# One of two small additions between two segments goes from VectorE to GpSimd, in a kernel whose order of work is written out by hand

## The chip, the cores and the metric

The kernel runs on one core of a Trainium2 chip. The metric is device time in microseconds (us) of one execution. Before the change three runs took 830.95, 831.56 and 833.34 us; the median is 831.56. One further execution was profiled: it took 830.06 us, and its span from the first to the last instruction is 828.3 us.

## The reference

Two attentions over the same 2048 rows of 512 values are mixed by a gate for each row. Part A is recurrent: the rows are cut into 64 segments of 32, and in front of each stand 8 memory rows, which are the first 8 output rows of the segment before it. Nothing of a segment that uses its memory rows can start before the segment before it has been projected out.

```python
mem = mem0                                     # (1, 8, 512)
for s in range(n_seg):                         # 64 segments of 32 rows
    h = jnp.concatenate([mem, x[:, 32*s:32*(s+1), :]], axis=1)
    q, k, v = (jnp.einsum('btd,dhe->bhte', h, W) for W in (Wq, Wk, Wv))   # 32 heads of 128
    scores = jnp.einsum('bhqe,bhke->bhqk', q, k) * scale
    p = softmax(jnp.where(mask, scores, -1e9))
    o = jnp.einsum('bhte,hed->btd', jnp.einsum('bhqk,bhke->bhqe', p, v), Wo)
    mem = o[:, :8, :]
    outs.append(o[:, 8:, :])
```

Part B is an attention over four blocks of 512 rows with 32 heads of 16, causal within a block, with a linear memory over the blocks before. The output is `g * a + (1 - g) * b`.

## The kernel before

**Start.** The first 60 us load the inputs, project part B for three of its four blocks, transpose x and store parts in DRAM. What follows, some 750 us, is the recurrence of part A with part B and the remaining work laid into its gaps.

**Order.** `A_ORDER` (L1069) is a text of 4589 units in the order in which they are recorded. Every unit is a small function that appends instructions to the queues of the engines; each engine then runs its own queue in that order, and semaphores hold it until its inputs are there. So the text sets the order on every engine at once. A `~` behind a unit that evacuates PSUM sends it to ScalarE instead of VectorE, or the other way (`evac`, L380 to L385).

**A segment.** In `segment(s)` the units are:
- `K0x` to `V1y`: the projections, by weight (K, Q, V), half of the heads (0, 1) and half of the contraction (x, y). Eight matmuls of 512 columns each (L1292); for Q1, sixteen of 256 (L1514). `k0`, `q0`, `v0` evacuate them and `TK0`, `TQ0` transpose (L1304).
- `Z`, `S`, `X`, `Y`, `M`, `L`, `N`, `n`: bias of the mask (L1560), scores (L1574), exponential (L1588), mask, sums (L1607), reciprocal (L1614, L1617), normalisation on VectorE (L1621) and of the memory rows on GpSimd (L1626).
- `PV`: probabilities times values (L1638, L1649). `E0` to `E3` evacuate it. `W0` to `W3` multiply by the output weights (L1375), sixteen matmuls each.
- `hm`: the memory rows for the next segment (`w_mem`, L1673). W leaves even and odd contributions in PSUM, in two halves of the partitions. A transpose (L1675) brings them into `tt`, a copy (L1676) brings partitions 64 to 127 of it to 0 to 63 in `tu`, and two additions (L1680, `hma` and `hmb`) of 64 partitions by 32 values write their sums into `xTp`: one for partitions 0 to 63, one for 64 to 127. All four are on VectorE. The first projection of the next segment waits for both additions.
- `H`, `ws`: the 32 output rows, evacuated and sent to DRAM.

**Work beside it.** `L` units are the projections of the memory rows' queries of four segments at a time, `O` their output parts, `T` the mix and the output of 128 rows (`T.b` is its matmul, L1455; `T.a` its sum on GpSimd, L1442). `pj` and `pp` project part B's fourth block. `bS` is two steps of part B's scores on TensorE (L932), `bE` an exponential on ScalarE (L953) followed by a causal select on GpSimd (L959), `bP` a step of its values (L985), `bT` the steps behind them (L1056 among them, on GpSimd). `oL` and `qt` are copies on GpSimd (L1704, L1727), `xl` too (L1317).

**GpSimd's queue.** `P.op` makes each GpSimd operation wait for the one before it (L116, L117). It runs strictly one after another in the recorded order.

A wait is recorded for the last writer of each tile that is read (`_mk_deps`); the two halves of a segment's memory rows are two names, `xu` and `xt`, and a projection reads both:

```python
rx = x_res(v, s // 16) + [Rs("xt%d" % s), Rs("xu%d" % s)]
```

Of the kernel before, what the change touches and what calls it, by code (L numbers as in the profile page):

```python
# [867 lines left out]
class BAttn:  # L868
# [210 lines left out]
    pj 2.E2~ pj pp pp 2.W0 2.W1 2.W2 2.W3 2.hm bP bS bP pj 3.qt pj 3.Q0x 3.Q0y bE bE 3.q0 bE 3.K0x~ 3.K0y 3.TQ0 3.K1x 3.K1y~ bE 3.Q1y 3.k0~ 3.TK0 3.Q1x
    3.S0 3.V0x 3.q1y~ 3.k1 3.TK1 1.ws 3.q1x 3.TQ1y 3.Z1 3.X0 2.H 3.TQ1x 3.V1x 3.Y0 3.S1~ bP 3.X1 3.M0 pp~ 3.V0y~ 3.L0 3.n0 3.M1 bP 2.oL bS 3.v0 3.L1 3.n1  # L1080
    3.V1y~ bE 3.N0 2.ws 3.N1 3.v1 pj bE pj 3.PV bT bE 3.E1~ L1.VL1x 3.E0~ L1.VL1y bE 3.W0 pp 3.E3 3.W1 3.E2~ 3.W2 L1.VL1e~ 3.W3 bS 4.qt 3.hm pj pj L1.VLt
    3.H bP pp bT bT bP bE bE 4.Q0x~ bE 4.Q0y~ 4.K0x~ 4.K0y~ bE 4.Q1y 4.q0~ 4.K1x 4.K1y 4.Q1x 4.k0~ bP 4.TK0 3.ws bP 4.TQ0 4.q1y~ 4.S0~ bS 4.k1 4.q1x~
    4.TK1 4.TQ1x 4.X0 L2.xl 4.V1x~ 4.TQ1y bE 4.Y0 4.Z1 bE 4.V1y~ 4.S1~ 4.M0 bE 4.X1 4.V0x~ 4.v1 4.V0y~ 4.M1 pj 4.L0 4.v0 pj 4.L1 pj 3.oL 4.n0 4.n1 4.N0
    4.N1 4.PV~ pj bE 5.Z1 4.E0 pp 5.qt 4.E1 bP 4.W0 pp~ 4.E2 4.W1 4.W2 4.E3~ 4.W3 bS~ bP O0.0 4.oL O0.1 4.hm bE 5.K0x~ 5.K0y~ bE bT 5.Q0x~ bE bE 5.k0
    5.Q0y~ 4.H 5.K1x~ 5.K1y 5.TK0 5.Q1y 5.q0~ 5.k1 bT 5.TQ0 5.TK1 5.Q1x 5.S0 5.V0x~ 5.q1y 5.q1x 5.TQ1y 5.TQ1x 5.X0 5.V0y 5.S1 5.X1 5.Y0 5.V1x~ 5.M0 5.V1y~
    5.L0 5.n0 5.M1 5.v0 O0.2 5.L1 5.v1 L2.KL1x 5.n1 5.N0 5.N1 O0.3 5.PV bP 5.E2~ 4.ws L2.KL1y~ O0.e bP 5.E0 6.qt bS~ 5.E1~ 5.W0 5.E3 L2.KL1e~ 5.W1 5.W2
    O0.s bE 5.W3 L2.KL0x 5.hm L2.KL0y~ bE bE bE bS~ bP 5.H bP 6.K0x~ 6.Q0x L2.KL0e bE bE bT bE 6.Q1y~ 6.K0y bE 6.k0~ 6.Q0y~ 6.Q1x~ 6.q1y~ 6.q1x~ 6.TQ1y
    6.TK0 bS~ bP 6.q0~ bP 6.K1x bE bE 6.TQ1x 6.TQ0 6.K1y 6.k1~ 6.TK1 6.V0x~ 6.S0~ 6.V1x~ bE 6.X0 6.Z1 6.Y0 bT 6.V0y~ bE 6.v0 6.S1 6.X1 6.M0 6.V1y~ 6.M1
    6.L0 6.n0 6.L1 bP 6.v1 bP bS~ 6.n1 5.oL 6.N0 6.N1 bE 6.PV~ bE 7.qt L2.QL1x bE bT 6.E0~ L2.QL1y 6.E1~ 6.E3 5.ws 6.E2 6.W0 L2.QL1e bE 6.W1 6.W2 6.W3 bP
    bP bS~ bE 6.hm L2.QL0x bE L2.QL0y 7.Q1x~ 7.K0x L2.QL0e 7.K0y~ 6.H bT 7.q1x~ bE 7.Q0x 7.k0 7.TK0 7.Q0y 7.K1x~ 7.K1y~ bE 7.q0~ 7.k1 7.TQ0 7.Q1y bP bP  # L1090
    7.q1y 7.S0 bS~ 7.TQ1x 7.TK1 7.X0 7.Z1 7.V1x 6.oL 6.ws 7.TQ1y bE bE bT 7.S1~ 7.V1y~ 7.X1 7.V0x bE 7.Y0 7.M0 7.V0y~ bT 7.M1 7.v1 7.L0 7.v0 7.N0 7.n0
    L2.VL0x 7.L1 L2.VL1x L2.VL0y 7.n1 7.N1 7.PV 7.E2~ L2.VL1y bE L2.VL0e~ 7.E1~ 7.E0 bP L2.VL1e 8.qt bP bS 7.W0 bE 7.E3 7.W1 7.W2 bE bE 7.W3 bE 8.Z1
    L2.VLt bS~ 7.hm 7.H bP bP bE bT bT bE 8.Q0x bE 8.Q0y 8.q0 8.K0x 8.K0y 8.K1x bE 8.k0 8.K1y 8.k1 8.TQ0 8.Q1y 8.TK0 8.Q1x 8.S0~ 8.V0x~ 8.V0y~ 8.q1y 8.TK1
    8.TQ1y 8.q1x 8.X0 8.TQ1x 8.S1 8.Y0 9.Z1 L3.xl 7.oL 8.X1 8.M0 8.v0 8.V1x 8.M1 8.V1y 8.L0 8.L1 8.N0 8.N1 L3.KL1x 7.ws 8.v1~ 8.n0 8.n1 O1.0 8.PV~ 8.E0
    8.E1~ 8.E3 bP L3.KL1y~ L3.KL1e 8.W0 9.qt 8.W1 8.E2 8.W2 8.W3 bP bS 8.hm 8.oL O1.1 O1.2 8.H bE 9.Q1x 9.K0x~ 9.K0y bE bE 9.Q0x~ 9.Q0y~ 8.ws 9.K1x~ bE
    9.k0~ 9.q1x 9.K1y~ bP 9.TQ1x 9.q0~ 9.Q1y 9.TK0 9.k1 9.TQ0 9.q1y 9.S0 9.TK1 9.TQ1y 9.V1x 9.V1y 9.X0 9.Y0 9.v1 9.S1~ 9.X1 bP 9.M0 9.L0 9.V0x~ 9.N0 9.M1
    9.L1 10.qt 9.n0 9.V0y~ O1.3 9.v0~ 9.N1 9.n1 O1.e~ L3.KL0x 9.PV bT 9.E0 9.E1~ 9.E3 bT L3.KL0y 9.W0 9.E2 9.W1 O1.s 9.W2 9.W3 11.Z1 bT bS~ 9.hm L3.QL0x
    L3.KL0e~ bE 10.Z1 L3.QL0y~ bE 10.K0x 10.Q0x~ bE 10.K0y~ 9.H 10.Q0y 10.K1x~ L3.QL0e 10.q0~ 10.k0~ 10.TQ0 10.K1y~ 10.Q1x~ 10.k1 10.Q1y 10.TK0 10.q1x
    9.oL 10.S0~ 10.V0x 10.TK1 10.q1y 10.TQ1x 10.V0y 10.X0 bE 10.TQ1y 10.S1 10.V1x 10.Y0 10.M0 9.ws 10.V1y~ 10.X1 10.L0 10.M1 10.L1 10.v0 T0.l 10.v1 10.N0
    L3.QL1x 10.n0 10.n1 10.N1 L3.VL0x L3.VL0y 10.PV bP 10.E0 L3.VL0e L3.QL1y 10.W0 10.E1 10.W1 10.E2 L3.QL1e~ 10.W2 10.E3~ 10.W3 10.hm bT bP bS T0.b bE  # L1100
    11.K0x~ bE 11.K0y~ 11.qt 11.Q0x~ 10.H 11.k0~ bE 11.Q0y~ bE 11.K1x~ 11.K1y 10.oL 11.Q1x~ T0.a 11.TK0 11.q0 11.TQ0 11.k1 11.TK1 11.q1x 11.Q1y~ 10.ws
    11.S0~ 11.q1y 11.TQ1x 11.V1x~ 11.X0 11.V0x 11.TQ1y 11.S1 T0.t 11.Y0 11.M0 bP 11.V0y~ 11.X1 11.L0 11.M1 bS 11.v0 11.L1 11.n1 11.N0 bP 11.N1 11.n0
    11.V1y bE L3.VL1x bE 11.v1 11.PV~ bE 11.E0 11.E1 11.E2~ 11.E3~ L3.VL1y 11.W0 L3.VL1e~ 11.W1 11.W2 11.W3 bE 11.hm 11.H L3.VLt bS 12.qt bP 11.ws bT bP
    bE bT bT bE 12.Q1x 12.K0x 12.K0y bE 12.Q1y bT 12.Q0x~ 12.q1x 12.Q0y 12.TQ1x bE bT 12.K1x~ 12.K1y~ 12.k0 bP bP bS~ 12.q1y L4.xl 12.q0~ 12.TK0 12.k1
    12.TQ0 bE 12.Z1 12.S0 12.X0 12.TQ1y bE 12.TK1 12.Y0 12.V0x~ 12.S1~ 12.V1x 12.M0 11.oL 12.V1y 12.X1 12.M1 12.V0y L4.KL1x 12.L0 12.L1 12.n0 12.v1 12.N0
    L4.KL1y 12.N1 T0.f 12.n1 12.v0~ 12.PV bE 12.E0 12.E3 L4.QL1x 12.E1~ 12.W0 12.W1 12.E2~ 12.W2 12.W3 L4.KL1e~ L4.KL0x 13.qt L4.KL0y 14.Z1 13.Z1 12.hm
    L4.KL0e~ L4.QL1y~ L4.QL1e~ 13.Q0x 13.Q0y~ 13.q0~ 13.K0x 12.H 13.K0y~ 13.TQ0 13.k0 bE 13.K1x 13.Q1x~ 13.q1x 13.TK0 13.K1y~ 13.S0~ 13.Q1y~ 13.TQ1x
    13.V1x~ 13.k1 13.TK1 13.q1y bP 13.V1y 13.TQ1y 13.S1~ 13.X0 bP 13.Y0 12.ws 13.M0 12.oL 13.V0x~ 13.X1 13.L0 13.M1 13.v1 13.n0 13.V0y O2.0 13.L1 13.N0
    13.n1 13.N1 O2.1 13.v0~ 13.PV L4.QL0x 13.E3~ 13.E1~ L4.QL0y 13.E0~ 13.W0 13.W1 13.E2~ L4.QL0e~ 13.W2 13.W3 bS 13.hm bE O2.2 bE bT bT 14.qt O2.3 14.K0x
    bE O2.e T1.l 14.Q0x 14.K0y~ 13.oL 14.Q0y bE 14.K1x 14.K1y~ 14.Q1x 14.k0~ 14.TK0 14.q0~ 14.TQ0 14.Q1y 14.S0 15.Z1 14.V1x 14.k1 14.q1x~ 14.TK1 14.V1y  # L1110
    14.TQ1x 14.q1y 14.TQ1y 14.S1 14.X0 T1.a 14.Y0 14.V0x 14.X1 14.M0 O2.s 14.V0y~ 14.M1 14.v1 13.H~ 14.L0 14.v0 L4.VL0x 14.N0 L4.VL0y 14.n0 14.L1 14.N1
    L4.VL1x 14.n1 14.PV~ L4.VL0e~ 14.E0 L4.VL1y 14.E1~ 14.E3 14.E2~ 13.ws L4.VL1e~ bT bT bT 14.W0 15.qt 14.W1 14.W2 14.W3 bP T1.b bP bS~ 14.hm 14.H bE bE
    15.Q0x 15.Q0y~ 15.q0 15.K0x~ T1.t bE 15.K0y~ 15.K1x 15.K1y~ 15.Q1y 15.TQ0 bE 15.k0~ 15.Q1x 15.k1 15.q1y 15.TK0 15.q1x 15.TK1 15.S0~ 15.V0x~ 15.X0
    15.TQ1y 15.TQ1x 14.oL 15.V0y 15.Y0 15.S1~ bP 15.M0 15.v0 15.V1x~ 15.X1 bP 15.M1 15.L0 15.L1 15.V1y 14.ws L5.xl 15.N0 15.v1 15.N1 15.n0 15.n1 bS bT bE
# [675 lines left out]
```

## Time and profile before

| | |
|---|---|
| median of three runs | 831.56 us (830.95 to 833.34) |
| profiled execution, its span | 830.06 us, 828.3 us |
| busy: TensorE, weight loads | 786.0 us, 486.1 us |
| busy: VectorE, ScalarE, GpSimd | 583.2, 562.7, 290.0 us |
| granted TensorE clock | 0.999 |
| the transpose in `hm` (L1675), 63 times | 450 ns each |
| the copy in `hm` (L1676), 63 times | 217 ns each |
| the two additions (L1680), 126 times | 207 ns each |

A busy time is the union of an engine's instructions. TensorE has two rows in the profile: PE, the matmuls, and PEld, the loading of the stationary operand, which runs ahead of the matmuls. In a group of instructions the columns are the busy time, the mean duration of one in ns, and the idle time of the engine just before them with what ended it. In a timeline the columns are the start and the duration in us.

### The profile page before, as it was taken

To read this page: it belongs to the slowest core of one execution; us is meant where nothing else is said; L and a number is where in the kernel's file an instruction comes from. 1 tells how busy PE (TensorE), PEld (TensorE's weight loads), DVE (VectorE), ACT (ScalarE), POOL (GpSimd) and SP (SyncE) were. 2 spreads that over 40 slices of the span, in tenths; PEclk is the share of its full clock that TensorE was granted. 3 is DMA by queue.
4 is the path that set the end of the run, shared out by engine and by line. 5 is a ranking of instruction groups with operands and counts; after the bars stand their busy time and mean duration, and the time that the engine had idled before them with its cause. 6 is when DMAs were issued, how large, how long until landed. Compare 5 with 4: busy or idle time off the path is not lost.

```text
span 828.3 us, 50504 instructions
## 1 busy us (share of the span) xinstructions
PE 786.0 (95%) x22701; PEld 486.1 (59%) x22707; DVE 583.2 (70%) x1486; ACT 562.7 (68%) x1353; POOL 290.0 (35%) x727
## 2 busy tenths in 40 slices
PE   9988999999999989999999999999999999999996
PEld 4644566656565656555556656556655656556565
DVE  4547676777677767787757677878667777787654
ACT  5544776867757677775767767776586685787543
POOL 4602442432435233242332434334133332454211
PEclk9999999999999999999999999999999999999999
DMA  8996332122213122112113122121312112120321
GB/s 330 417 377 193 97 94 70 53 50 69 65 59 82 30 63 61 48 34 79 51 49 91 32 60 70 25 62 41 88 57 62 54 59 65 33 72 17 87 87 59
DMA packets 100596, 72.28 MB, mean 87 GB/s; under 512 B 58036, under 2 KB 94492, under 8 KB 98844
## 3 DMA queue, kind: packets, MB, share of 16 engines
q1 hardware_dynamic: 99676, 68.24, 26.9%
q8 instruction: 178, 2.92, 1.5%
q10 hardware_dynamic: 704, 0.80, 0.3%
q14 instruction: 38, 0.31, 0.1%
HBM read 43.43 MB, written 25.58 MB: 83 GB/s over the span
## 4 chain that ended last, share of the span: by engine, by line
PE 77%; ACT 7%; DVE 6%; POOL 3%; DMA 3%; issue 3%; SPq 0%; DVEq 0%; POOLq 0%; ACTq 0%
PE ps L1292 38%; PE ps L1375 15%; PE ps L1514 6%; PE ps L1638 3%; PE ps L932 2%; PE ps L985 2%; ACT PTT L953 2%; POOL PTT L959 2%; DMA scr_kqd<-stgk 2%; PE ps L698 1%; PE ps L1574 1%; PE ps L1455 1%; DMA Wv_sb<-in_A_Wv_dram 1%; PE ps L1607 1%; ACT R_sb L1617 1%
## 5 line engine op out<-in xcount | busy, mean ns | idle before, releaser
L953 ACT ACTIVATE PTT<-ps 128x512 bf16<-128x512 f32 x320 | 172.2, 602 | 51.9 <-PE ps L932 37.6
L959 POOL TENSOR_SCALAR_AFFINE_SELECT PTT<-PTT 128x128 bf16<-128x128 bf16 (+2 forms) x320 | 121.2, 379 | 242.2 <-ACT PTT L953 223.5
L1292 PE MATMUL ps<-Wv_sb,xTp 128*32 128x512 bf16 x2048 | 145.4, 382 | 0.4 <-issue 0.4
L1292 PE MATMUL ps<-Wk_sb,xTp 128*32 128x512 bf16 x2048 | 133.3, 379 | 1.3 <-DVE xTp L1680 0.9
L1375 PE MATMUL ps<-Wo_sb,OT_sb 128*32 128x256 bf16 x4096 | 125.6, 273 | 9.4 <-ACT OT_sb L383 4.6
L1375 PEld LDWEIGHTS ps<-Wo_sb,OT_sb 128*32 128x32 bf16 x4096 | 104.3, 97 | 32.7 <-ACT OT_sb L383 23.0
L1626 POOL TENSOR_TENSOR P_sb<-P_sb,R_sb 128x64 bf16<-128x64 bf16 x128 | 50.3, 393 | 170.5 <-ACT R_sb L1617 165.4
L1292 PEld LDWEIGHTS ps<-Wk_sb,xTp 128*32 128x32 bf16 x2048 | 57.0, 97 | 51.1 <-DVE xTp L1680 5.8
L383 ACT ACTIVATE QN_sb<-ps 128x256 bf16<-128x256 f32 (+1 forms) x152 | 67.3, 445 | 28.1 <-PE ps L1292 23.2
L383 ACT ACTIVATE OT_sb<-ps 128x320 bf16<-128x320 f32 x157 | 59.0, 438 | 30.6 <-PE ps L1649 29.2
L383 ACT ACTIVATE KN_sb<-ps 128x512 bf16<-128x512 f32 x88 | 52.8, 600 | 31.1 <-PE ps L1292 30.4
L385 DVE CAST V_sb<-ps 128x512 bf16<-128x512 f32 x82 | 56.0, 685 | 24.3 <-PE ps L1292 22.7
L1514 PE MATMUL ps<-Wq_sb,xTp 128*32 128x256 bf16 x2048 | 72.1, 273 | 0.7 <-DVE xTp L1680 0.5
L1304 DVE STREAM_TRANSPOSE KT_sb<-KN_sb 128x256 f32<-128x256 f32 x128 | 55.9, 437 | 21.6 <-ACT KN_sb L383 17.6
L1292 PE MATMUL ps<-Wq_sb,xTp 128*32 128x512 bf16 x1024 | 70.6, 379 | 0.4 <-DVE xTp L1680 0.3
L1304 DVE STREAM_TRANSPOSE QT_sb<-QN_sb 128x128 f32<-128x128 f32 (+1 forms) x192 | 63.1, 335 | 8.2 <-ACT QN_sb L383 6.4
L1588 ACT ACTIVATE P_sb<-ps 128x224 bf16<-128x224 f32 x128 | 45.7, 357 | 32.3 <-PE ps L1579 30.9
L1675 DVE STREAM_TRANSPOSE tt<-ps 128x256 f32<-128x256 f32 x63 | 28.4, 450 | 53.6 <-PE ps L1375 52.8
L1514 PEld LDWEIGHTS ps<-Wq_sb,xTp 128*32 128x32 bf16 x2048 | 55.4, 97 | 17.4 <-DVE xTp L1680 3.9
L385 DVE CAST OT_sb<-ps 128x320 bf16<-128x320 f32 x99 | 44.6, 485 | 24.8 <-PE ps L1649 23.6
L1292 PEld LDWEIGHTS ps<-Wv_sb,xTp 128*32 128x32 bf16 x2048 | 44.7, 100 | 14.3 <-issue 1.6
L1621 DVE TENSOR_TENSOR P_sb<-P_sb,R_sb 128x160 bf16<-128x160 bf16 x128 | 40.2, 330 | 12.1 <-ACT R_sb L1617 11.5
(146 smaller groups left out, 1409.9 us busy)
## 6 DMA issues: line engine op xcount, KB each, us to landing
scr_aTd<-WN SPq DMA_DIRECT2D x63, 128.0 KB, 2.4
AR<-scr_aTd SPq DMA_DIRECT2D x60, 96.0 KB
Wk_sb<-in_A_Wk_dram SPq DMA_DIRECT2D x4, 1024.0 KB, 10.4
Wq_sb<-in_A_Wq_dram SPq DMA_DIRECT2D x4, 1024.0 KB, 13.9
Wv_sb<-in_A_Wv_dram SPq DMA_DIRECT2D x4, 1024.0 KB, 13.5
Wo_sb<-in_A_Wo_dram SPq DMA_DIRECT2D x8, 512.0 KB, 6.2
scr_vld<-VNL SPq DMA_DIRECT2D x16, 256.0 KB, 2.3
VL<-scr_vld SPq DMA_DIRECT2D x64, 64.0 KB
```

The costliest lines, as they stand in the source:

```text
L383: P.op("act", lambda a: a.activation(dst, src, ACT.Copy), reads=[v.rbank[k] for k in bks], writes=dres, name=name)
L385: P.op("dve", lambda d: d.tensor_copy(dst, src), reads=[v.rbank[k] for k in bks], writes=dres, name=name)
L953: P.op("act", lambda a: a.activation(pt, v.pb[bk], ACT.Exp, scale=v.SCALE_B), reads=[v.rbank[bk]], writes=[rp], name="be%d_%d" % (n, t))
L959: P.op("gp", lambda g: g.affine_select(mv, mv, [[0, len(cut)], [1, 128]], ALU.is_ge, 0.0, base=0, channel_multiplier=-1), reads=[rp], writ ...
L1292: ins = pe.matmul(pb[bk][SEG * j:SEG * (j + 1), :], lhs(c), cols(w, j) if split else w[:, 512 * j:512 * (j + 1)], start=(c == 0), stop=(c ...
L1304: P.op("dve", lambda d: d.transpose(to, src), reads=reads, writes=writes, name=name)
L1375: ins = pe.matmul(pb[bk][SEG * j:SEG * (j + 1), 0:256], lhs(h), Wo_sb[:, h, :].rearrange("p (k q c) -> p q k c", q=2, c=64)[:, j % 2], sta ...
L1514: ins = pe.matmul(pb[bk][SEG * j:SEG * (j + 1), 0:256], lhs(c), cols(w_sb[:, c, 2048 * b + 1024 * half:2048 * b + 1024 * (half + 1)], j), ...
L1588: P.op("act", lambda a: a.activation(P_sb[:, b, :], pb[bk][:, 0:So], ACT.Exp, scale=SCALE), reads=[rbank[bk]], writes=[Rs("Pm%d" % b), Rs( ...
L1621: P.op("dve", lambda d: d.tensor_tensor(wide[b][:, :, 0:L], wide[b][:, :, 0:L], R_sb[:, b, :].rearrange("p (i q) -> p i q", q=L), ALU.mult ...
L1626: P.op(ENG["n"], lambda d: d.tensor_tensor(left, left, grp04(R_sb[:, b, :]), ALU.mult), reads=[Rs("R0_%d" % b)], writes=[Rs("PL%d" % b)], ...
L1675: P.op("dve", lambda d: d.transpose(v.tt[:, :, :].rearrange("p (k n) t -> p k n t", n=2), src), reads=[rbank[wb["bk"]]], writes=[Rs("tt")] ...
```

## The change

In `w_mem` the second of the two additions is recorded for GpSimd instead of VectorE. Its operands are the same. The transpose, the copy and the first addition stay on VectorE.

```diff
             for b in range(2):
                 dst = xTp[64 * b:64 * b + 64, :, SEG * (s + 1):SEG * (s + 1) + M].rearrange("p (a n) t -> p a n t", n=2)
                 one, two = (t[0:64, :, 0:M].rearrange("p (a b n) t -> p b a n t", a=2, b=2)[:, b] for t in (v.tt, v.tu))
-                P.op("dve", lambda d, dst=dst, one=one, two=two: d.tensor_tensor(dst, one, two, ALU.add), reads=[Rs("tt"), Rs("tu")], writes=[Rs("x%s%d" % ("ut"[b], s + 1))], name="hm%s%d" % ("ab"[b], s))
+                P.op(("dve", "gp")[b], lambda d, dst=dst, one=one, two=two: d.tensor_tensor(dst, one, two, ALU.add), reads=[Rs("tt"), Rs("tu")], writes=[Rs("x%s%d" % ("ut"[b], s + 1))], name="hm%s%d" % ("ab"[b], s))
```

`A_ORDER` is a new text. It has the same 4589 units, apart from the `~` marks (902 before, 886 after), in another order from its fourth line on. As an example, this is what stands between `W3` and the first projection of the next segment at three of the 63 boundaries:

```diff
-28.W3 L8.KL1y~ bS 28.hm bP O6.0 28.H bE L8.KL1e bE bE bT 29.Q1y~
+28.W3 28.hm L8.KL0e~ L8.KL1e~ bS~ bT 29.Z1 bP O6.0 28.H bE bE 29.Q1y~
-46.W3 bS 47.Z1 L12.QL1x L12.QL1y~ bE 46.hm 47.K0x
+46.W3 47.qt bT bS~ 47.Z1 46.hm L12.QL1y~ bE L13.xl 47.K0x~
-56.W3 L15.KL1x 56.hm bT bT L15.KL1y~ L15.KL0e~ bP bP bS 56.H L15.KL1e~ 57.Q0x~
+56.W3 bT bP L15.KL1y 56.hm bS L15.KL0e~ 56.H L15.KL1e~ bT bP 57.K0x
```

Counted over all 63 boundaries, the units between `W3` and the first projection are, before and after: half projections of `L` 58 and 54, `O` 35 and 34, `pj` 7 and 6, `T.b` 9 and 9, `bS` 50 and 50, `bP` 58 and 47, `Z` 28 and 23. Between `W3` and `hm` alone, `bE` stands 28 times before and 20 times after. Between the last of `V0y` and `V1y` and `PV`, half projections of `L` are 74 before and 80 after.

More of the change, by code (lines that the diff above doesn't have):

```diff
@@ L1079 @@
[L1079 to L1114, printed above, removed]
@@ L1256 @@
+    63.K0y 63.Q0y 63.Q1y 62.ws 63.k0~ 63.K1x O15.s 63.K1y 63.q0~ 63.TK0 T15.l 63.q1y 63.V0x~ 63.TQ1x 63.TQ0 63.k1~ 63.S0~ 63.TK1 63.V1x~ 63.V0y~ 63.X0
+    63.Y0 63.M0 63.TQ1y 63.S1~ T14.t 63.L0 63.V1y 63.v0 63.X1 63.v1~ 63.n0 63.M1 63.L1 T14.f 63.N0 63.n1 T15.b 63.N1 63.PV~ 63.E0 63.E1 63.E3 63.E2 T15.a
+    63.W0 63.W1 63.W2 63.W3 T15.t 63.H T15.f
 """
```

325 lines of the change are left out of this document (179 added, 146 removed).

## The prediction

> **What bounds the kernel now.** I read the page's busy table first, then the chain that ended last, then the groups by line, and then one segment boundary in the timeline.
>
> ```profile
> span 828.3 us, 50504 instructions
> PE 786.0 (95%) x22701; PEld 486.1 (59%) x22707; DVE 583.2 (70%) x1486; ACT 562.7 (68%) x1353; POOL 290.0 (35%) x727
> PE 77%; ACT 7%; DVE 6%; POOL 3%; DMA 3%; issue 3%; SPq 0%; DVEq 0%; POOLq 0%; ACTq 0%
> L1680 DVE TENSOR_TENSOR xTp<-tt,tu 64x32 bf16<-64x32 f32 x126 | 26.0, 207 | 3.0
> ```
>
> TensorE is busy for 786.0 of 828.3 us, so all its idle time is 42.3 us, and no cheaper vector operation can win more than that. The two additions together cost VectorE 26.0 us, but VectorE holds only 6% of the chain that ended last. What counts is when they end, because the first projection of the next segment waits for them. The view of one line shows who waited:
>
> ```profile
> L1680 DVE TENSOR_TENSOR xTp<-tt,tu x126: 182/184/1260, 76.0 to 812.4; 64x32 bf16<-64x32 f32 x126
>   PEld ps L1292: 9.8, 29
>   PEld ps L1514: 3.9, 10
> ```
>
> Weight loads waited 13.7 us in all, at 39 of 63 boundaries. That is the pot that a shorter chain can draw on; part of it hides behind the last matmul still running. One boundary in the timeline:
>
> ```profile
> 399.61 0.50 PE L1375 MATMUL ps<-Wo_sb,OT_sb 128*32 128x256 bf16 x12
> 399.83 0.11 PEld L985 LDWEIGHTS ps<-PTT,Vj 128*32 128x32 bf16 x4
> 400.16 0.45 DVE L1675 STREAM_TRANSPOSE tt<-ps 128x256 f32<-128x256 f32 x1 [1.34 <-PE ps L1375]
> 400.48 0.55 PEld L1455 LDWEIGHTS ps<-woB_sb,oTg 128*32 128x32 bf16 x16 [0.21 <-issue]
> 400.65 0.19 DVE L1676 COPY tu<-tt 64x64 f32<-64x64 f32 x1
> 400.87 0.38 DVE L1680 TENSOR_TENSOR xTp<-tt,tu 64x32 bf16<-64x32 f32 x2
> 401.31 0.26 PEld L1514 LDWEIGHTS ps<-Wq_sb,xTp 128*32 128x32 bf16 x12 [0.28 <-DVE xTp L1680]
> ```
>
> The last output matmul ends at 400.11. Transpose, copy and two additions run to 401.25, and the projection starts at 401.31: 1.20 us in which TensorE has only what the order puts between W3 and the next segment's first projection. I call that the cover.
>
> **The change part by part.**
>
> *The addition (hmb) moves to GpSimd.* Before, the later addition ends 0.41 us after the copy (400.84 to 401.25). After, it needs a hand-over from VectorE to GpSimd and GpSimd's own duration:
>
> ```profile
> 351.16 0.48 DVE L1054 SCALAR_TENSOR_TENSOR oTt<-oTt,gBp 128x256 f32<-128x256 f32 x1
> 351.73 0.73 POOL L1056 TENSOR_TENSOR orow<-adot,oTt 128x256 bf16<-128x256 f32 x1 [2.80 <-DVE oTt L1054]
> L407 POOL COPY gBp<-gB_sb 32x8 f32<-32x8 f32 x4 | 0.8, 188 | 10.1 <-DVE gB_sb L613 9.9
> L1626 POOL TENSOR_TENSOR P_sb<-P_sb,R_sb 128x64 bf16<-128x64 bf16 x128 | 50.3, 393 | 170.5 <-ACT R_sb L1617 165.4 <-POOL OTL L1704 0.2
> 408.09 0.31 POOL L1626 TENSOR_TENSOR P_sb<-P_sb,R_sb 128x64 bf16<-128x64 bf16 x1 [0.18 <-ACT R_sb L1617]
> 408.34 0.58 DVE L1621 TENSOR_TENSOR P_sb<-P_sb,R_sb 128x160 bf16<-128x160 bf16 x2
> 408.65 0.45 POOL L1626 TENSOR_TENSOR P_sb<-P_sb,R_sb 128x64 bf16<-128x64 bf16 x1 [0.25 <-ACT R_sb L1617]
> ```
>
> The hand-over is 0.09 us (351.64 to 351.73). The trace has no GpSimd addition of 32 elements. From below it is bounded by the copy of 8 elements, 0.19; from above by the mean of the one with 64, 0.39. The unhindered one with 64 takes 0.31 and the one with 256 takes 0.73, so 0.42/192 = 2.2 ns an element, and 32 elements come to 0.31 - 0.07 = 0.24 us. I take 0.24. hmb then ends 0.09 + 0.24 = 0.33 us after the copy instead of 0.41, and the whole chain falls from 1.20 to about 1.11 us (1.06 to 1.27 with the two ends). No row shows a GpSimd operation that reads partitions 0 to 63 and writes 64 to 127, as this one does; I take no surcharge, and a surcharge lies inside the upper end. TensorE now waits for two semaphores at that place; the first is done earlier and I cost the second at nothing, with 0.05 us more if it isn't.
>
> Does the addition beside it hinder it? In the last three rows the first GpSimd addition has VectorE's two-input multiply only near its end and takes 0.31; the second starts while L1621 runs (to 408.92) and takes 0.45, so it ends 0.18 after L1621's end. The first addition on VectorE starts 0.03 after the copy and ends 0.21 after it. A hindered GpSimd addition of 64 elements would end 0.18 later, at 0.39; one of 32, less 0.07, at 0.32. That is no later than the unhindered 0.33. So side by side costs nothing by these rows.
>
> By the Trainium skill, "SBUF — State Buffer", section "Who interferes with whom", a VectorE instruction with two SBUF inputs and a GpSimd instruction that reads SBUF exclude each other for the whole instruction. That the trace shows exclusion agrees (0.31 against 0.45), but the 0.18 shows that only the part after the start-up has to wait; taken whole, the rule gives the rival on the lock below.
>
> *VectorE is freed.* 63 additions at 207 ns are 13.0 us of VectorE time. I take 0: the evacuation that follows the pair waits for the projection on TensorE, not for VectorE. Without that cover it could give back up to 1 us of the 3.0 us idle that L1680 itself met.
>
> *GpSimd gets* 63 x 0.24 = 15 us more, 35% to 37% busy. Behind hmb in its queue stand causal selects (L959), which the values matmuls of part B (L985) wait for, the copies of left queries and outputs, and the small normalisations. hmb waits for VectorE's copy and holds these up. I take 0: the idle before the normalisations alone is 170.5 us.
>
> *The new order.* Counting units between each W3 and the next segment's first projection, 63 boundaries: half projections and output parts of four loads per tile (L, O, pj) fall from 100 to 94, bP from 58 to 47, bias units Z from 28 to 23; bS (50) and T.b (9) stay. Slots:
>
> ```profile
> 76.82 2.62 PE ps L1292 x48
> 396.72 0.11 PEld L1560 LDWEIGHTS ps<-mbias,id 128*32 128x32 bf16 x4
> ```
>
> Eight projection matmuls fill 2.62/6 = 0.44 us, a Z and a small bP 0.11 each. So cover falls by 6 x 0.43 + 11 x 0.11 + 5 x 0.11 = 4.3 us; summed unit by unit it goes from 70.1 to 65.8 us. It shrinks at 22 boundaries and grows at none. Taking 1.20 less the cover wherever it is positive, the old order leaves 8.0 us uncovered (43 boundaries). The new one leaves 7.3 us if the chain is 1.11, 5.5 if it is 1.06, 11.1 if it is still 1.20, 14 to 15 if it is 1.27. Term: -0.7 us, ends -2.5 and +6.5.
>
> The 4.3 us taken from the boundary stand elsewhere, since the total work is the same. Mostly they are now between the value projections and PV: half projections from 74 to 80 there. What waits there:
>
> ```profile
> PEld ps L1638 <- ACT V_sb L383: 23.0, 43, 1.2
> PEld ps L1638 <- DVE P_sb L1621: 5.1, 11, 0.8
> PEld ps L1607 <- ACT P_sb L1588: 16.9, 51, 0.8
> ```
>
> PV waits at 43 of 64 segments for the evacuation of V, 0.53 us each as weight loads see it. Cover there is worth at most its length, 4.3 us, and at least nothing, since the normalised probabilities (L1621) come almost as late and end the wait next. I take 1.8, a little under the middle.
>
> *Sum:* -0.7 - 1.8 = -2.5 us. The profiled execution took 830.06 us (span 828.3 and 1.8 around it), so 827.6. The runs' median is 831.56, 1.5 above it, which gives 829.0 on the scale of the result.
>
> **The rivals.**
>
> *The lock is whole* (about +3 us). If hmb can start only when VectorE's addition has ended, it ends 0.21 + 0.24 = 0.45 us after the copy, the chain is 1.24, and the new order leaves 13.1 us against 8.0: +5.1 - 1.8 = +3.3 on 831.6, so 834.9. Against it stands the 0.45 of the blocked row, which a whole lock would have made 0.27 + 0.31 = 0.58.
>
> By the Trainium skill, "GPSIMD Engine Reference", section "Engine selection", a two-input elementwise operation is about twice as slow there as on VectorE; that would make hmb an estimated 0.37 us and the chain much as in this rival. The rows of this case give 0.24.
>
> *hmb queues behind selects* (slower, about +4 us; the other side of my forecast). GpSimd works in order. In the new order 20 bE units stand between W3 and hm, at 13 boundaries (up to four at one); each is an ACT exponential followed by a select, and hmb, unlike the VectorE addition, can't pass the select:
>
> ```profile
> L953 ACT ACTIVATE PTT<-ps 128x512 bf16<-128x512 f32 x320 | 172.2, 602 | 51.9 <-PE ps L932 37.6
> POOL PTT L959 <- ACT PTT L953: 223.5, 179, 6.6
> 352.62 1.27 POOL L1442 TENSOR_TENSOR aTg<-AR 128x512 bf16<-128x512 f32 x1 [0.17 <-POOL orow L1056]
> 352.68 1.46 DVE L1680 TENSOR_TENSOR xTp<-tt,tu 64x32 bf16<-64x32 f32 x2
> ```
>
> If ACT is one exponential late (0.60) at 11 of the 13, TensorE waits 6.6 us more: 6.6 - 2.5 = +4.1, 835.7. It decides from 2.5/13 = 0.19 us at each of them. For it: the selects wait for ACT 179 times already. Against it: the old order has 28 such bE, the new one fewer, and ACT is 68% busy. The last two rows show the same thing on VectorE: a GpSimd sum in progress stretched the pair from 0.38 to 1.46. Such meetings are at 12 boundaries now, they hit either place, and I keep them equal.
>
> *The order gains more than I count* (-6 us, 825.5): the full 4.3 us of moved cover works and the chain is 1.06.
>
> *The change doesn't do what it says:* the chain is no shorter, and what the order loses at the boundary (11.1 - 8.0 = 3.1) it wins back elsewhere (1.8): +1.3 us, 832.9, no change.
>
> **How the numbers follow.** About 0.3%, 2.5 us, is what a measurement of this kernel can tell from no change. The forecast (829.0, itself from -5 to 0 us) gets 0.47: 0.28 of it faster, 0.19 same. More gain 0.12, faster. The lock 0.09 and the queue 0.22, slower but for 0.02 that counts as same. The change without effect 0.10: 0.06 same, 0.04 slower. Faster 0.40, same 0.27, slower 0.33. The range goes from 824.0 (the larger gain and 1.5 us of scatter) to 837.0 (the two slower rivals, 834.9 and 835.7, and 1.3 us of scatter).
>
> **What would show each step.** In the changed profile: L1680 on POOL x63 at about 240 ns, 200 to 300 if I am right, over 370 if it is blocked whole; its start 0.09 us after the copy's end, far later at boundaries with a late select; the wait of the projections' weight loads for xTp near 13 us in all, named POOL; and the wait of L1638 for V below 23.0 us. Wrong it would be if that wait doesn't fall, if the waits of L1292 and L1514 for xTp rise by 5 us, or if other evacuations come later because their engines were swapped: the marks for that changed all over the order, and I have counted them at nothing.

## The result, and the profile after

The changed kernel takes 823.49 us, median of four runs (821.48 to 823.71); the kernel before took 832.13 beside it (830.95 to 833.34, four runs). The ratio is 0.9891, 95% interval 0.9869 to 0.9913. It is faster, by 7 to 11 us. The forecast was 829.0, and the range ended at 824.0. Two later measurements of the same kernel gave 0.9917 (0.9891 to 0.9943) and 0.9919 (0.9899 to 0.9938), so some 7 us is the better figure: the direction was right, the size nearly three times the forecast, and 823.49 lies just below the range. The profiled execution took 823.53 us.

The page of the kernel after, its busy table and the shares of the chain that ended last:

```profile
span 821.8 us, 50553 instructions
PE 783.3 (95%) x22701; PEld 489.3 (60%) x22707; DVE 567.1 (69%) x1428; ACT 559.4 (68%) x1348; POOL 306.1 (37%) x790
PE 79%; DVE 6%; ACT 6%; DMA 3%; issue 2%; POOL 2%; SPq 1%; ACTq 0%; DVEq 0%; POOLq 0%
```

GpSimd has its 16 us more, VectorE 16 us less, and TensorE's idle time (span less PE) went from 42.3 to 38.5 us. Next, the view of the line of the two additions in the kernel after, with what waited for it:

```profile
L1680 DVE TENSOR_TENSOR xTp<-tt,tu x63: 182/183/324, 75.6 to 806.1; 64x32 bf16<-64x32 f32 x63
L1680 POOL TENSOR_TENSOR xTp<-tt,tu x63: 244/253/455, 75.8 to 806.1; 64x32 bf16<-64x32 f32 x63
  DVE tu L1676: 139.5, 58
  PEld ps L1292: 9.5, 30
  PEld ps L1514: 2.4, 8
```

The addition on GpSimd takes 253 ns in the middle of the 63, where 240 was forecast. At 58 of 63 boundaries the copy on VectorE was the last thing it waited for, so GpSimd was free there. Weight loads wait 11.9 us for it, against 13.7 before. The boundary that the prediction showed, in the timeline after:

```profile
398.10 0.39 PE L1375 MATMUL ps<-Wo_sb,OT_sb 128*32 128x256 bf16 x8
...
398.54 0.45 DVE L1675 STREAM_TRANSPOSE tt<-ps 128x256 f32<-128x256 f32 x1 [0.41 <-PE ps L1375]
...
399.02 0.19 DVE L1676 COPY tu<-tt 64x64 f32<-64x64 f32 x1
399.25 0.18 DVE L1680 TENSOR_TENSOR xTp<-tt,tu 64x32 bf16<-64x32 f32 x1
399.29 0.26 POOL L1680 TENSOR_TENSOR xTp<-tt,tu 64x32 bf16<-64x32 f32 x1 [0.80 <-DVE tu L1676]
...
399.62 0.20 PEld L1292 LDWEIGHTS ps<-Wk_sb,xTp 128*32 128x32 bf16 x8
```

From the start of the transpose to the end of the later addition it is 1.01 us (398.54 to 399.55), where it was 1.09 (400.16 to 401.25). Over all 63 boundaries the median went from 1.09 to 1.01 by the same reading. The hand-over, 399.21 to 399.29, is 0.08 us. The two additions run side by side, and GpSimd's takes 0.26: no lock is to be seen.

So the shorter chain that the forecast is built on is there to the hundredth. Whether it makes the gain is another question, and the matmuls' own waits are a first hint. In a row of the waits view stand the total, the number of waits and the longest one. These are the rows of the waits view for PE in the kernel before:

```profile
PE ps L1292 <- DVE xTp L1680: 1.2, 3, 0.7
PE ps L1514 <- DVE xTp L1680: 0.5, 2, 0.3
PE ps L1638 <- ACT V_sb L383: 3.1, 6, 0.8
PE ps L985 <- POOL PTT L959: 2.8, 7, 0.7
```

and in the kernel after:

```profile
PE ps L1292 <- POOL xTp L1680: 0.6, 3, 0.3
PE ps L1638 <- ACT V_sb L383: 2.0, 4, 0.8
PE ps L985 <- POOL PTT L959: 2.2, 5, 0.7
```

The weight loads' 13.7 us shrink to 1.7 us of matmul idle (1.2 + 0.5, at five boundaries): while a weight load waits, the matmuls issued ahead of it are still running. The view leaves out short gaps; TensorE's whole idle time ahead of L1292 and L1514, whatever ended it, is 3.5 us. By these readings a shorter chain alone could win 1.7 to 3.5 us, and 1.1 of the 1.7 went.

### The profile page after: what moved, and what is told of

Same layout as the page of the kernel before. It is cut to its first block, busy times and chain, and to the rows that moved or that the text cites. A ratio compares the mean times of both kernels' runs of the same rounds, so it can differ in the third digit from the quotient of the medians.

```text
span 821.8 us, 50553 instructions
## 1 busy us (share of the span) xinstructions
PE 783.3 (95%) x22701; PEld 489.3 (60%) x22707; DVE 567.1 (69%) x1428; ACT 559.4 (68%) x1348; POOL 306.1 (37%) x790
## 3 DMA queue, kind: packets, MB, share of 16 engines
q8 instruction: 178, 2.92, 1.6%
## 4 chain that ended last, share of the span: by engine, by line
PE 79%; DVE 6%; ACT 6%; DMA 3%; issue 2%; POOL 2%; SPq 1%; ACTq 0%; DVEq 0%; POOLq 0%
PE ps L1292 38%; PE ps L1375 16%; PE ps L1514 6%; PE ps L1638 3%; PE ps L932 2%; PE ps L985 2%; PE ps L698 2%; PE ps L1455 2%; PE ps L1574 1%; DVE V_sb L385 1%; POOL PTT L959 1%; PE ps L1607 1%; DMA Wv_sb<-in_A_Wv_dram 1%; ACT PTT L953 1%; DVE P_sb L1621 1%
## 5 line engine op out<-in xcount | busy, mean ns | idle before, releaser
L1292 PE MATMUL ps<-Wv_sb,xTp 128*32 128x512 bf16 x2048 | 144.7, 383 | 0.1
L1292 PE MATMUL ps<-Wk_sb,xTp 128*32 128x512 bf16 x2048 | 134.0, 379 | 0.3 <-POOL xTp L1680 0.3
L1375 PEld LDWEIGHTS ps<-Wo_sb,OT_sb 128*32 128x32 bf16 x4096 | 104.9, 97 | 27.6 <-ACT OT_sb L383 20.9
L383 ACT ACTIVATE QN_sb<-ps 128x256 bf16<-128x256 f32 (+1 forms) x146 | 64.4, 446 | 35.5 <-PE ps L1292 30.2
L1292 PEld LDWEIGHTS ps<-Wk_sb,xTp 128*32 128x32 bf16 x2048 | 57.6, 97 | 47.1 <-POOL xTp L1680 4.7
L383 ACT ACTIVATE OT_sb<-ps 128x320 bf16<-128x320 f32 x163 | 61.4, 439 | 32.7 <-PE ps L1649 32.1
L385 DVE CAST V_sb<-ps 128x512 bf16<-128x512 f32 x85 | 57.9, 686 | 26.2 <-PE ps L1292 24.6
L1514 PE MATMUL ps<-Wq_sb,xTp 128*32 128x256 bf16 x2048 | 72.7, 273 | 0.1
L1292 PE MATMUL ps<-Wq_sb,xTp 128*32 128x512 bf16 x1024 | 71.0, 380 | 0.9 <-ACT WN L383 0.4
L1680 POOL TENSOR_TENSOR xTp<-tt,tu 64x32 bf16<-64x32 f32 x63 | 16.6, 264 | 140.2 <-DVE tu L1676 139.5
L1514 PEld LDWEIGHTS ps<-Wq_sb,xTp 128*32 128x32 bf16 x2048 | 55.3, 97 | 17.0 <-POOL xTp L1680 2.4
L1588 ACT ACTIVATE P_sb<-ps 128x224 bf16<-128x224 f32 x128 | 45.6, 357 | 26.2 <-PE ps L1579 22.6
L385 DVE CAST OT_sb<-ps 128x320 bf16<-128x320 f32 x93 | 42.6, 485 | 26.1 <-PE ps L1649 25.1
L1292 PEld LDWEIGHTS ps<-Wv_sb,xTp 128*32 128x32 bf16 x2048 | 45.6, 100 | 14.0 <-issue 0.9
## 6 DMA issues: line engine op xcount, KB each, us to landing
Wk_sb<-in_A_Wk_dram SPq DMA_DIRECT2D x4, 1024.0 KB, 10.2
Wq_sb<-in_A_Wq_dram SPq DMA_DIRECT2D x4, 1024.0 KB, 13.7
```

Source lines behind the costliest of these rows:

```text
L383: P.op("act", lambda a: a.activation(dst, src, ACT.Copy), reads=[v.rbank[k] for k in bks], writes=dres, name=name)
L385: P.op("dve", lambda d: d.tensor_copy(dst, src), reads=[v.rbank[k] for k in bks], writes=dres, name=name)
L1292: ins = pe.matmul(pb[bk][SEG * j:SEG * (j + 1), :], lhs(c), cols(w, j) if split else w[:, 512 * j:512 * (j + 1)], start=(c == 0), stop=(c ...
L1375: ins = pe.matmul(pb[bk][SEG * j:SEG * (j + 1), 0:256], lhs(h), Wo_sb[:, h, :].rearrange("p (k q c) -> p q k c", q=2, c=64)[:, j % 2], sta ...
L1514: ins = pe.matmul(pb[bk][SEG * j:SEG * (j + 1), 0:256], lhs(c), cols(w_sb[:, c, 2048 * b + 1024 * half:2048 * b + 1024 * (half + 1)], j), ...
L1588: P.op("act", lambda a: a.activation(P_sb[:, b, :], pb[bk][:, 0:So], ACT.Exp, scale=SCALE), reads=[rbank[bk]], writes=[Rs("Pm%d" % b), Rs( ...
```

## The experiments

Each ratio is to the kernel before, run beside the kernel in question. The expectations, printed as they stood before each run, use labels: f1 is the order alone run again and f2 the changed kernel beside it; e6 and f4 are the changed kernel with a shift of TensorE's instructions, f3 the order alone with it; e7 is the changed kernel with eight units moved.

### The two parts of the change, one at a time

The line alone; the text of the order is the old one:

```diff
-                P.op("dve", lambda d, dst=dst, one=one, two=two: ...
+                P.op(("dve", "gp")[b], lambda d, dst=dst, one=one, two=two: ...
```

> The old order with the second addition on GpSimd, nothing else. Theory A, the line itself carries the gain (a chain of 1.11 instead of 1.20 us, and GpSimd's copies can no longer run into the pair because hmb stands in GpSimd's queue): by the old order's cover 8.0 - 5.3 = 2.7 us less is uncovered, and 2 to 2.5 us of the 3.9 us that TensorE waited at stretched pairs goes, so 4 to 5 us faster than before. Theory B, the new order carries the gain: within 2 us of before, or slower where hmb queues behind the 28 selects that stand between W3 and hm in the old order.

Measured: 848.36 us, ratio 1.0223 (1.0200 to 1.0247), before 830.69. The line alone costs 17.7 us. Its matmul waits:

```profile
PE ps L1292 <- POOL xTp L1680: 12.5, 13, 1.9
PE ps L985 <- POOL PTT L959: 6.5, 10, 1.5
PE ps L1514 <- POOL xTp L1680: 1.9, 4, 0.8
POOL xTp L1680 <- DVE tu L1676: 99.3, 41, 4.7
```

The three PE rows sum to 20.9 us, where the kernel before has 4.5 (1.2 + 0.5 + 2.8): 16.4 us more. The profiled execution was the longest of its five (852.8 us), and its span is 22.6 us above the one before (850.9 against 828.3), so these rows are most of the loss and not all of it. The last row says why: only at 41 of 63 boundaries does GpSimd wait for the copy; at the others it is held by something else. One of these in the timeline of this kernel:

```profile
494.21 0.19 DVE L1676 COPY tu<-tt 64x64 f32<-64x64 f32 x1
494.44 0.18 DVE L1680 TENSOR_TENSOR xTp<-tt,tu 64x32 bf16<-64x32 f32 x1
...
494.84 0.29 POOL L959 TENSOR_SCALAR_AFFINE_SELECT PTT<-PTT 128x128 bf16<-128x128 bf16 x1 [4.15 <-ACT PTT L953]
495.32 0.29 POOL L959 TENSOR_SCALAR_AFFINE_SELECT PTT<-PTT 128x128 bf16<-128x128 bf16 x1 [0.19 <-ACT PTT L953]
495.76 0.72 POOL L1056 TENSOR_TENSOR orow<-adot,oTt 128x256 bf16<-128x256 f32 x1
...
496.63 0.24 POOL L1680 TENSOR_TENSOR xTp<-tt,tu 64x32 bf16<-64x32 f32 x1
496.93 0.12 PEld L1292 LDWEIGHTS ps<-Wq_sb,xTp 128*32 128x32 bf16 x8 [2.33 <-POOL xTp L1680]
```

The copy is done at 494.40. Two selects, each behind its exponential, and an output sum of part B (L1056) stand ahead in GpSimd's queue, and the addition starts at 496.63. A pair on VectorE would have been done at about 494.8.

The order alone; the text of the order is the new one, and the line stays:

```diff
                 P.op("dve", lambda d, dst=dst, one=one, two=two: ...
```

> The new order with both additions on VectorE. Theory A: the chain is 1.20 us again, cover is 4.3 us shorter than in the old order, so 11.1 - 8.0 = 3.1 us more is uncovered, less 1.8 us won elsewhere: 0 to 3 us slower than before. Theory B: at least half of the gain stays, 4 to 7 us faster than before.

Measured: 825.38 us, ratio 0.9933 (0.9917 to 0.9949). The order alone is worth 5.6 us (4.2 to 6.9 by the interval), where the fourth rival had it at +1.3. With the line's +17.7 the two parts are far from adding up. What the order was to lose at the boundary it did not lose; this is the only row in which its matmuls wait for the additions, where it was 1.7 us before:

```profile
PE ps L1292 <- DVE xTp L1680: 1.1, 5, 0.3
```

To split the gain on one chip, the order alone and the changed kernel ran side by side; the changed kernel had been run a second time before, too.

> The new order with both additions on VectorE, again, beside the changed kernel: ratio to before 0.992 to 0.995. If the addition on GpSimd is worth the 3.8 us that the forecast gave it within the new order, this one is 3 to 4.5 us above f2. If it is worth what the weight loads' waits show (12.0 against 5.0 us at the boundaries, of which the delayed addition gave back 4.3 us for 7.7 us of wait, so a good half), it is 3.5 to 4 us too; if it is worth the difference of the two profiled idle times of TensorE (38.1 against 37.5 to 38.5) it is 0 to 1 us.

> The changed kernel beside f1: ratio to before 0.989 to 0.992.

> The changed kernel itself, run again beside the three others: 821 to 825, ratio to before 0.988 to 0.993. It is the mark for e7, and beside the order alone it gives what the second addition on GpSimd is worth in the new order: -1.9 us if the two medians of the earlier sessions hold (825.4 and 823.5).

Measured: order alone 825.28 us, 0.9934 (0.9915 to 0.9952); changed 824.61, 0.9919 (0.9899 to 0.9938); the earlier second run 822.69, 0.9917. So within the new order the addition on GpSimd is worth 0.7 us on this chip, and no more than some 2 us over all runs (the mean of the three ratios of the changed kernel, 0.9909, against 0.9934). The 3.8 us of the forecast's term are more than either leaves room for; of the three readings named in the expectation, TensorE's idle time was the right one and the weight loads' waits the wrong one.

### Is it GpSimd's queue?

If the selects ahead of the addition make the 17.7 us, the memory rows must go ahead of them. Old order, with `hm` directly behind `W3` at all 63 boundaries, on GpSimd and, as the control, on VectorE:

```diff
-0.W3 bE pj 0.hm bE pj pp bP
+0.W3 0.hm bE pj bE pj pp bP
```

> The old order with the second addition on GpSimd, and with the unit of the memory rows moved directly behind the last output part at all 63 boundaries (54 of them move), so that no causal select of that stretch stands ahead of the addition in GpSimd's queue. TensorE's order is the old one, unchanged. Theory (the 17.7 us that the line costs in the old order are GpSimd's queue: 28 selects ahead of the addition): it falls from 848.4 to between 828 and 834, and lies within 2.5 us of the same kernel with both additions on VectorE. Rival (the operation on GpSimd beside VectorE's is itself what costs, or the queue of GpSimd is full anyway): it stays above 838.

> Control of the run before: the same order, the unit of the memory rows directly behind the last output part, both additions on VectorE. VectorE now waits for the last output part before evacuations that stood ahead of it, so it may lose. Expected 829 to 834 (the kernel before 830.7); 835 or more would say that the place of the unit costs VectorE something by itself, and then the run before is to be read against this one and not against the kernel before.

Measured: 851.15 us, 1.0253 (1.0233 to 1.0274) on GpSimd; 836.33, 1.0074 (1.0058 to 1.0091) on VectorE. My theory failed by its number: the time did not fall at all. The control, too, came out above the 829 to 834 expected, so the place of the unit costs 6.2 us by itself, and the two are to be read against each other. The matmul waits of the kernel on GpSimd tell why it failed:

```profile
PE ps L985 <- POOL PTT L959: 16.6, 13, 3.0
PE ps L1292 <- POOL xTp L1680: 1.7, 3, 0.7
```

The projections' wait is gone (14.4 to 2.3 us with L1514's 0.6), and part B's wait for the selects has come in its place, 6.5 to 16.6. The same queue blocks in the other direction, as in this stretch of its timeline:

```profile
266.69 0.45 POOL L1680 TENSOR_TENSOR xTp<-tt,tu 64x32 bf16<-64x32 f32 x1 [2.67 <-DVE tu L1676]
266.75 0.28 DVE L1004 TENSOR_SCALAR pQj<-pQj 128x512 bf16<-128x512 bf16 x1
267.27 1.51 POOL L959 TENSOR_SCALAR_AFFINE_SELECT PTT<-PTT 128x384 bf16<-128x384 bf16 x2
268.84 0.25 PEld L985 LDWEIGHTS ps<-PTT,Vj 128*32 128x32 bf16 x12 [3.24 <-POOL PTT L959]
```

GpSimd sits 2.67 us on the addition, waiting for the copy; the selects behind it start only at 267.27, and TensorE stands until 268.84. In the control on VectorE the same row is small:

```profile
PE ps L985 <- POOL PTT L959: 1.9, 5, 0.7
```

The two kernels differ by 14.8 us, these waits (L985 and xTp, 18.9 against 2.9) by 16.0, and their profiled spans by 16.5. Not all of that is idle time of TensorE: its idle time is 12.4 us more and its busy time 4.1, at a granted clock of 0.991 against 0.997, and why that clock is lower here stays open. So the cost in the old order is in the main GpSimd's queue, whichever stands first; it is not the speed of the addition there.

The same was tried on the changed kernel, to gain what is left at its late boundaries: `hm` first at 0, 7, 51, 55 and 56, and the unit with VectorE's L1004 later at four others.

```diff
-51.W3 bE bT bE bE 51.hm bS~ 52.Z1
+51.W3 51.hm bE bT bE bE bS~ 52.Z1
```

> The changed kernel with eight units of the order moved, TensorE's order unchanged: at segments 0, 7, 51, 55 and 56 the memory rows stand directly behind the last output part, ahead of the selects, and at 19, 26, 43 and 50 the unit that issues VectorE's in-place minimum of part B stands some units later, so that it no longer runs beside the addition on GpSimd. Theory (what is left of the boundary wait in the changed kernel, 5.0 us in all, comes in part from these nine late additions): GpSimd's addition takes 0.25 to 0.28 us at those four boundaries instead of 0.45, and the time falls by 0.5 to 1.7 us. Rival (these waits are covered, or the held selects give it back): within 0.5 us of the changed kernel, or slower by up to 2 us, since the old order with the rows first only moved the wait from the projections to part B.

Measured: 832.10 us, 1.0030 (1.0006 to 1.0053): 9 us lost; the profiled execution, 828.09, is one of its shortest. At 19, 26 and 50 the addition on GpSimd takes 0.25 us again; at 43 L1004 still starts beside it, and it still takes 0.45. A gain from that can't be seen: up to segment 48 the profile lies within 0.7 us of that of the changed kernel run beside it, while two other profiles of that kernel differ from it by up to 1.4 and 3.7 us there. From 48 to 57, where the rows stand first at 51, 55 and 56, it loses 6 us, and the wait of L985 for the selects rises from 2.5 to 6.8, as here:

```profile
677.17 0.25 POOL L1680 TENSOR_TENSOR xTp<-tt,tu 64x32 bf16<-64x32 f32 x1 [1.43 <-DVE tu L1676]
677.56 1.48 POOL L959 TENSOR_SCALAR_AFFINE_SELECT PTT<-PTT 128x256 bf16<-128x256 bf16 x3
679.09 0.23 PEld L985 LDWEIGHTS ps<-PTT,Vj 128*32 128x32 bf16 x12 [2.20 <-POOL PTT L959]
```

So at some boundaries that look late the selects are better first.

Two further runs put an operation of one column into GpSimd's queue. In the first (old order, additions on VectorE) it waits behind the pair, so that nothing recorded later on GpSimd starts beside the pair:

```diff
+            P.op("gp", lambda gq: gq.memset(v.scr[:, :], 0.0), deps=[Rs("xt%d" % (s + 1)).w], writes=[Rs("scr")], name="bar%d" % s)
```

> The old order with both additions on VectorE, and behind them a GpSimd memset of one value to a spare tile that waits for the second addition; TensorE doesn't wait for it. It costs about 0.11 us of GpSimd and keeps what is recorded behind it out of the pair. Theory A (collisions of GpSimd's copies with the pair cost TensorE time): the pair is stretched at 4 or fewer boundaries instead of 12, the longest addition under 0.5 us, and the time is 2 to 3 us below before. The rival, that these collisions were hidden: within 1 us of before, or slower by what the memset holds up.

Measured: 836.34 us, 1.0072 (1.0049 to 1.0095). The pair was still stretched at 12 boundaries, as before, because the GpSimd operations that meet it are recorded ahead of `hm`; and holding GpSimd's queue cost 5.6 us by itself (the wait of L985 for the selects is 7.9 us here against 2.8). In the second, the changed kernel has the operation between copy and addition, so that the addition comes later:

```diff
+            P.op("gp", lambda gq: gq.memset(v.scr[:, :], 0.0), deps=[Rs("tu").w], writes=[Rs("scr")], name="dly%d" % s)
```

> The changed kernel with a GpSimd memset of one value to a spare tile between the copy and hmb, so that hmb starts about 0.16 us later: the chain is about 1.27 us instead of 1.11. By the cover count of the new order 14.6 - 7.3 = 7 us more is uncovered: 5 to 8 us slower than the changed kernel if the end of hmb is what TensorE waits for at nearly all boundaries; 0 to 2 us if other waits stand right behind it.

Measured: 827.80 us, 0.9958 (0.9943 to 0.9974), some 4 us above the changed kernel (0.9909) and 2.4 above the order alone, which ran beside it. The addition ends 0.15 us later. A later chain does cost, by an amount between the two cases expected. Its matmul waits for xTp account for 1.5 us (2.1 against 0.6), all idle time ahead of L1292 and L1514 for 2.6 to 2.8 (5.0 against 2.2 to 2.4 in three profiles of the changed kernel); the rest stays open:

```profile
PE ps L1292 <- POOL xTp L1681: 1.6, 6, 0.3
PE ps L985 <- POOL xTp L1681: 0.3, 1, 0.3
PE ps L1514 <- POOL xTp L1681: 0.2, 1, 0.2
L1681 POOL TENSOR_TENSOR xTp<-tt,tu x63: 244/245/296, 76.2 to 810.7; 64x32 bf16<-64x32 f32 x63
```

The last row is also a control for the lock: in this kernel GpSimd's addition starts behind the end of VectorE's at all 63 boundaries, and it takes 245 ns alone, against 253 beside it.

### Where in the order the gain lies

Both additions on VectorE; new and old order change places between the value matmuls of segment 19 and those of 34, where both texts have used up the same units.

```diff
 0.PV ... 19.PV      old order
-19.PV ... 34.PV     old order
+19.PV ... 34.PV     new order
 34.PV ... 63.PV     old order
```

The second kernel is the counterpart, with the new order outside and the old one inside.

> Both additions on VectorE; the old order, but with the new order's units from behind the value matmuls of segment 19 to those of segment 34 (1054 of 4589 units, a quarter). Theory (the order's gain sits there: in the profiles the lead of the new order grows by 3.0 us between these two places, of 4.6 in all): 826.5 to 828.5. Rival (the gain is spread evenly, what the profiles show is one execution's chance): a quarter of 5.3 us, so 829 to 830.

> The counterpart: both additions on VectorE, the new order, but with the old order's units in that stretch. Theory (the gain sits in the stretch): 828 to 829.5, most of the gain gone. Rival (spread evenly): 826 to 827, three quarters of it kept.

Measured: 827.17 us, 0.9970 (0.9954 to 0.9986) with the new order inside; 827.45, 0.9980 (0.9961 to 0.9998) with it outside. That is 2.5 us and 1.7 us below the kernel before, together 4.2, against 5.5 for the whole. The quarter inside may hold more than its share (1.4), but the intervals, 1.2 to 3.8 us and 0.2 to 3.2 us, are too wide to choose between the two theories; the times that both had named stood for a kernel before at some 831 us, and it was at 829.03 here. Each part gains something, so the gain is not in one place alone.

### Where TensorE's instructions fall

In both profiles weight loads wait now and then with no releaser, as here in the kernel before, the longest:

```profile
424.50 0.12 PEld L1375 LDWEIGHTS ps<-Wo_sb,OT_sb 128*32 128x32 bf16 x7 [1.31 <-issue]
```

Counting TensorE's instructions from the start, I found 27 such waits over 0.15 us at places 187 and 188 of each 256, give or take one, 13.5 us in all; after, 24 with 11.6 us. The count takes in all of TensorE's records, the 260 of its semaphore waits and drains too; by weight loads and matmuls alone, as the expectation below has it, the places scatter. A new order moves what stands at those places, which could make or hide a gain. Three wide and 48 narrow warm-up matmuls instead of seven wide ones move everything by 88 places:

```diff
-        for n in range(WARM):
-            ins = pe.matmul(v.pb[bk], v.warm[:, 0:128], v.warm[:, :], start=True, stop=True)
+        for n in range(51):
+            ins = pe.matmul(v.pb[bk], v.warm[:, 0:128], v.warm[:, :], start=True, stop=True) if n < 3 else pe.matmul(v.pb[bk][0:1, 0:1], v.warm[:, 0:1], v.warm[:, 0:1], start=True, stop=True)
```

> The kernel before with the seven warm-up matmuls at its start replaced by three of them and 48 of one column, so that every later TensorE instruction (matmuls and weight loads counted) stands 88 places further on; nothing else differs. In the profiles the weight loads wait without a releaser near places 187 and 188 of each 256, 27 such waits over 0.15 us with 13.5 us in the kernel before. Theory (TensorE's instructions come in blocks of 256, and a late block costs by what stands there): the waits stay at places 187 and 188 and so hit other matmuls, the sum of them stays between 10 and 17 us, the 1.31 us at 424.5 us on the output matmuls goes, and the time changes by up to 3 us in either direction: 827.5 to 833.5. Rival (the places are a coincidence of the program): the waits stay at the same matmuls, now at places 19 and 20, and the time is that of before within 1 us.

> The changed kernel with the same shift by 88 TensorE instructions. If the gain of the change is the order and the shorter chain, e6 stays 6 to 10 us below the shifted kernel before: 821 to 826. If the gain came in good part from where the blocks of instructions happen to end in the one order and in the other, the gap between the two shifted kernels leaves 6 to 10 us, towards 3 to 5.

> The new order with both additions on VectorE and TensorE's instructions shifted by 88 places. If the share of the addition does not hang on the placement, f3 stands as far above f4 as f1 above f2, within 1 us.

> The changed kernel with the same shift, again: ratio to before 0.991 to 0.995, 0 to 2 us above f2.

Measured: before with the shift 832.04 us, 1.0021 (1.0005 to 1.0037); changed with the shift 824.41, 0.9930 (0.9913 to 0.9948), and again 826.44, 0.9939 (0.9919 to 0.9960); order alone with the shift 826.23, 0.9945 (0.9926 to 0.9965). The waits stayed at the same places of the 256, one earlier (186 and 187; these traces lack one matmul record more), and so met other matmuls, and the 1.31 us at 424.5 us went; their sum was 7.9 us in the shifted kernel before, below the 10 to 17 expected, and 9.6 in the shifted changed one. The time moved by 1 to 2 us, not by their sum and not with its sign. The gain stays: shifted against shifted it is 0.9930/1.0021 = 0.9909 for the change (0.9918 by its second run) and 0.9945/1.0021 = 0.9924 for the order alone. The addition on GpSimd is worth nothing here (0.9939 against 0.9945, side by side).

## Why the prediction was right and wrong

**Right: the duration, the hand-over, the chain.** The addition takes 253 ns where 240 was forecast, the hand-over 0.08 us for 0.09, and the chain is shorter by 0.08 us where 0.09 was forecast. Side by side with VectorE's addition it takes 253 ns against 245 alone; the rival of the whole lock is false. At four boundaries (19, 26, 43, 50) VectorE's next instruction did hold it, as in this timeline after:

```profile
305.43 0.18 DVE L1680 TENSOR_TENSOR xTp<-tt,tu 64x32 bf16<-64x32 f32 x1
305.48 0.45 POOL L1680 TENSOR_TENSOR xTp<-tt,tu 64x32 bf16<-64x32 f32 x1 [0.64 <-DVE tu L1676]
305.53 0.28 DVE L1004 TENSOR_SCALAR pQj<-pQj 128x512 bf16<-128x512 bf16 x1
```

It takes 0.45 us and ends 0.12 after L1004, the one-input minimum of 512 bf16 values that stands behind VectorE's addition; where L1004 was moved away from it (19, 26 and 50 in the run with eight units moved), it took 0.25. By the Trainium skill, "SBUF — State Buffer", section "Who interferes with whom", such a `tensor_scalar` can enter a two-port mode and then excludes GpSimd. The trace agrees on that; that whoever issues first gets the ports is not what its recorded starts show, since GpSimd's starts 0.05 us earlier and still ends last.

**Right by its number, wrong in its parts: the boundary.** The term was -0.7, made of +3.1 for the order and -3.8 for the chain. With the addition on GpSimd, the idle time ahead of L1292 and L1514 fell from 3.5 to 2.3 us in the first two profiles. That the number is near is luck. The order alone, which was to lose 3.1 us there, lost next to nothing (3.5 and 4.0 us of that idle time in its two profiles, and 1.1 us of matmul waits for xTp against 1.7). The chain, which was to give 3.8, took that idle time from there to 2.2 to 2.4; in time it gave 0.7 us beside the order alone and nothing with the shift, where the idle time is 3.3 us without it and 3.1 and 3.4 with it. The step that failed here is "taking 1.20 less the cover wherever it is positive": it takes TensorE to stand as soon as the units between are used up. Much of that time is covered: the weight loads wait while the matmuls ahead of them still run. The profile had said so, in the PE rows of the waits view, which I did not read: 1.7 us.

**Wrong in size: what the order gives elsewhere.** This is the step that put the time below the range. "The 4.3 us taken from the boundary stand elsewhere ... I take 1.8", and "counted at nothing" for the marks that changed with the order. In the forecast the order as a whole costs 1.3 us (3.1 lost, 1.8 won) and the chain makes the gain; measured, the order is worth 5.5 us and the chain 0 to 2. So the kernel became faster, as forecast, but for another reason; the rival in which the order gains more (825.5) came nearest, though by other ways than its chain of 1.06. The named place did what was said, for less. In groups by line, the row of L1638 before and after (its columns are busy time, mean ns, and idle time ahead with what ended it):

```profile
L1638 PE MATMUL ps<-P_sb,V_sb 32*128 32x40 bf16 x2048 | 24.9, 176 | 11.0 <-ACT V_sb L383 3.1 <-DVE P_sb L1621 2.9 <-ACT PTT L953 2.0
```

```profile
L1638 PE MATMUL ps<-P_sb,V_sb 32*128 32x40 bf16 x2048 | 25.2, 177 | 9.9 <-DVE P_sb L1621 4.0 <-ACT V_sb L383 2.0 <-DVE oTt L1024 0.8
```

V's wait falls by 1.1 us and that for the normalised probabilities, as forecast, takes it up by 1.1; what else ended waits there fell too, and the sum is 1.1 us less. It is 10.6 to 11.0 in the six profiles in which TensorE has the old order and 9.5 to 10.2 in the eight of the two kernels with the new order as it stands and of their shifted forms, so this part is not chance. The scores (L1574) stand idle 1.0 to 1.4 us in these eight, against 0.2 in the kernel before and in its shifted form. TensorE's whole idle time is 42.3 and 41.6 us in these two, 37.5 to 40.8 in the eight, 39.1 on average: 2.9 us less. Another part, 1.7 us, is in PE's busy time, 784.1 on average against 785.8; there the same kernel differs by 2.0 us between two executions (783.3 and 785.3), so what is behind it cannot be read from profiles. Which of the order's moves make the 5.5 us stays open, beyond the 1.1 us of idle time at PV: the exchange of the stretches says only that they are in more than one place.

**The queue.** I gave this rival 0.22 and 6.6 us, from 13 boundaries with selects ahead. In the new order it hardly acts: the addition stands late behind selects at four boundaries (0, 7, 51 and 55). The mechanism is real all the same, and larger than I had it: with the old order the line costs 17.7 us. So the new order is needed for the line to be harmless, while the line adds little to the order. That the meetings of GpSimd operations with the pair "hit either place" was wrong too: something stretched the chain at 12 boundaries before and at 9 after, for the most part others, by my count of the timelines, and at 7 with the order alone.

**The signs.** The weight loads' wait for xTp (11.9 us, named POOL) and PV's wait for V (20.1 us, below 23.0) came as the prediction said they would if it was right. They show that the pieces behaved as drawn, not where the gain came from.

## What to carry to other kernels

Read how much a chain costs from the idle time of the matmuls (PE), not from that of the weight loads (PEld), which run ahead of them: here 1.7 us against 13.7. Add the short gaps that the waits view leaves out, and take the sum as a guide only: the delayed addition cost some 4 us with 2.6 to 2.8 us of that idle time. Before a small operation goes to an engine with an in-order queue, look at what stands ahead of it and what comes to stand behind it; either can cost far more than the operation saves. When a change holds a line and a new order, price the order by itself, as it may be nearly all of the gain, while the line by itself, in the old order, does harm.
